# A fused attention and mixer kernel: scores with 128 instead of 112 stationary columns of k, and k kept ahead of q in its tile

## The chip, the cores and the metric

The kernel runs on one core of a Trainium2 chip. The metric is the device time of one execution in microseconds; the time of a kernel is the median of its runs. The page called "the profile" describes one such execution, taken by the hardware profiler: its span goes from the first to the last instruction. PE is TensorE's matmul stream, PEld its weight loads, DVE is VectorE, ACT is ScalarE, POOL is GpSimd and SP is SyncE, which issues most of the DMAs.

## The reference

Two layers follow each other. The first is attention with normalised queries and keys, over 8 batches of 12 heads with 448 positions and 64 channels a head:

```
q_n, k_n = rmsnorm(q, g_q), rmsnorm(k, g_k)          # over the 64 channels
scores   = q_n @ k_n^T / 8                            # 448 x 448 for each head
attn     = exp(scores - max) / (sum(exp(...)) + 1e-9)
x        = attn @ v                                   # heads side by side: 448 x 768 a batch
```

The second is a mixer over `x`: a low-rank mixing of the positions (`U` is 448 x 32, `V` is 32 x 448), then a two-layer perceptron over the channels:

```
u   = x + (x^T @ U @ V)^T
out = u + relu(u @ w_ch1) @ w_ch2                     # 768 -> 3072 -> 768
```

## The kernel before

The 448 positions of a head are laid on 112 partitions with four positions each (`SP = 112`, `NJ = 4`). A group `t` is four heads (24 groups in all), a pair `p` is two heads (48 pairs, six a batch). Pairs are the unit of attention: the 64 channels of the first head lie on partitions 0 to 63 and those of the second on 64 to 127.

For a group, `load` (L187) brings q and k by SP's DMA queue, `squares` (L217, ScalarE or GpSimd) and `reduce` (L227, VectorE) form the sums of squares, `rsqrt` (L234, ScalarE) their inverse roots, and `scale` (L239, VectorE) writes the normalised q and k of one pair as bfloat16 into a tile `qkn`. The index `s` runs over the two tensors in all of them. `transposes` (L250) turns `qkn` into `qkT`, a tile of 128 partitions by 2 by 448: for the first `NPE = 14` pairs by eight TensorE transposes and two VectorE evictions (L258 multiplies q by the gains, L259 copies k), and for later pairs by a DMA transpose (L261), after which `gains` (L263) multiplies q in place.

`scores` (L267) takes chunks of 112 keys as the stationary operand and all 448 queries as the moving one. For each chunk `kc` it issues two weight loads and two matmuls, one for each head of the pair, on the two halves of the partitions; each head has a PSUM bank of its own in the tile `sc` (two tiles of two banks each, pool `ps_s`). `expo` (L277) has ScalarE take the exponential of both heads at once, from PSUM to the bfloat16 tile `E`, one instruction for each chunk. `values` (L281) multiplies `E` (112 keys by 128 queries as the stationary operand) by v with a column of ones appended, so that the last column of the result is the sum of the exponentials; VectorE takes its reciprocal and scales (L302 to L306). The maximum isn't subtracted.

The mixer follows for each batch: `mix_t` and `mix_u` (L317 to L339) for the low-rank part, where `mix_t` uses 32 stationary columns, then `mlp` (L471). Its first product (`ph`, L477) has 128 x 128 stationary tiles of `w1b` and 384 or 512 moving columns; ScalarE and VectorE share the evictions with the relu (L480, L482). The second (L404, tiles `po`, `pa`, `pb`, `pe`) works on 384 columns at a time, with sums and differences of blocks so that seven products do for eight.

The order of the work is written out by hand. `head` (L573) issues the loads, the set-up and all of batch 0's attention; there `scores` is called for single chunks, and short runs of unused matmuls (`heat`, L737) fill gaps on TensorE. From then on `weave` (L725) interleaves the perceptron of batch `b` with the attention of batch `b + 1`: the perceptron is a generator that yields after each block of TensorE work, and each item of `attention` (L505) has a weight that says how much of that work goes before it. There `scores` is called with two chunks at a time, twice a pair, and its four matmuls stand between blocks of the perceptron. The last batch's perceptron has nothing woven in. Each engine works through its instructions in the order in which they were issued.

Of the kernel before, what the change touches and what calls it, by code (L numbers as in the profile page):

```python
# [9 lines left out]
FP32 = mybir.dt.float32  # L10
# [3 lines left out]
OP = AluOpType  # L14
# [3 lines left out]
def kernel(  # L18
# [13 lines left out]
    nc = tc.nc  # L32
    B, H, S, D = q.shape
# [5 lines left out]
    P = 128  # L39
    NJ = 4  # L40
    SP = S // NJ
# [4 lines left out]
    PAD = 64  # L46
# [21 lines left out]
    ps_s = ctx.enter_context(tc.tile_pool(name="ps_s", bufs=2, space=bass.MemoryType.PSUM))  # L68
# [17 lines left out]
    gg = consts.tile([P, 1], FP32, name="gg")  # L86
# [25 lines left out]
    def E_of(p):  # L112
        return Es[p % 3 if p < 6 else p % 2]
# [71 lines left out]
    qks, vts, sqs, rstds, qkns, qkTs, scs, x3_of = {}, {}, {}, {}, {}, {}, {}, {}  # L185

    def load(t, parts=1, ss=(0, 1)):  # L187
        b, h0, n = t // 3, (t % 3) * HG, HG // parts
        for s in ss:
            if t in (2, 3):  # L190
                qks[t, s] = spare[0:SP, t - 2, s]
            elif (t, s) in ((1, 1), (5, 1)):
                qks[t, s] = k1
            else:
                qks[t, s] = loads.tile([SP, HG, NJ * D], FP32, tag="qk", name="qk", bufs=3)
        for h in range(0, HG, n):
            for s in ss:
                nc.sync.dma_start(qks[t, s][:, h:h + n],
                                  (q, k)[s][b, h0 + h:h0 + h + n].rearrange("h (p j) d -> p h (j d)", j=NJ))

    def load_v(t):
        b, h0 = t // 3, (t % 3) * HG
# [47 lines left out]
    def transposes(p):  # L250
        qkn = qkns[p].rearrange("p s j h d -> p (s j) (h d)")
        qkT = attn.tile([P, 2, S], BF16, tag="qkT")
        qkTs[p] = qkT
        if p < NPE:
            pt = ps_mm.tile([P, 2, S], BF16, tag="mm")
            for i in range(2 * NJ):
                nc.tensor.transpose(pt.rearrange("d s (j p) -> d (s j) p", j=NJ)[:, i, :], qkn[:, i, :], ident[:SP, :SP])
            nc.vector.tensor_scalar(qkT[:, 0], pt[:, 0], gg, None, OP.mult)  # L258
            nc.vector.tensor_copy(qkT[:, 1], pt[:, 1])  # L259
        else:  # L260
            nc.sync.dma_start_transpose(qkT.rearrange("d s (j p) -> d (s j) p", j=NJ), qkn)  # L261

    def gains(p):  # L263
        if p >= NPE:
            nc.vector.tensor_scalar(qkTs[p][:, 0], qkTs[p][:, 0], gg, None, OP.mult)  # L265

    def scores(p, kcs):  # L267
        qT, kT = qkTs[p][:, 0], qkTs[p][:, 1]
        for kc in kcs:
            sc = ps_s.tile([SP, 2, 512], FP32, tag="s")  # L270
            for hh in range(2):
                pp = slice(hh * D, (hh + 1) * D)
                nc.tensor.matmul(sc[:, hh, 0:S], kT[pp, kc * SP:(kc + 1) * SP], qT[pp, :],  # L273
                                 start=True, stop=True)
            scs[p, kc] = sc

    def expo(p, kc):  # L277
        nc.scalar.activation(E_of(p)[:, :, PAD + kc * S:PAD + (kc + 1) * S], scs.pop((p, kc))[:, :, 0:S],  # L278
                             AF.Exp, scale=float(D) ** 0.5)

    def values(p, hh):  # L281
# [223 lines left out]
    def attention(b, extra={}):  # L505
# [11 lines left out]
        for p in range(b * 6, b * 6 + 6):  # L517
            t, odd = divmod(p, 2)
            more, more2 = t + 1 < NT, t + 2 < NT
            add(2 if p == 6 else 1, scores, p, (0, 1))  # L520
            add(0, expo, p, 0)
            add(.5, expo, p, 1)
            if p + 1 < NP and (p + 1 >= NPE or not odd):
                add(.5, transposes, p + 1)
# [16 lines left out]
            if odd and p > 6:  # L541
                if 6 <= t + 2 < NT:
                    add(0, load, t + 2, 1, (1,))
                    add(0, load_v, t + 2)
                if t + 3 < NT:
                    add(0, load, t + 3, 1, (0,))
            add(1, scores, p, (2, 3))
            add(0, expo, p, 2)
            add(.5, expo, p, 3)
            if p + 1 < NPE and odd:  # L550
                add(.5, transposes, p + 1)
            if 7 <= p <= 10:
                add(0, mix_u, 0, p - 7, (1,))
            if p + 1 < NP:
                add(0, gains, p + 1)
# [17 lines left out]
    def head():  # L573

        A, Bh = slice(0, 2), slice(2, 4)
        load(0, 2)
        load(1)
        load(2)
# [16 lines left out]
        gain()  # L595
        reduce(0, Bh, (1,))
        transposes(0)
        heat(3)
        squares(1, ALL, (0,), nc.gpsimd)
        rsqrt(0, Bh)  # L600
        scores(0, (0, 1))
        fill = {n: [] for n in range(24)}

# [184 lines left out]
```

## Time and profile before

| | |
|---|---|
| median of 4 runs | 587.05 us (586.18 to 592.49) |
| profiled execution, whole time | 592.49 us |
| its span, from the first to the last instruction | 590.70 us |
| TensorE matmuls (PE) busy | 570.6 us, 97% of the span, 4613 instructions |
| weight loads (PEld) busy | 315.6 us, 4613 instructions |
| VectorE, ScalarE, GpSimd busy | 397.6, 279.7, 77.3 us |
| score matmuls (L273) | 384, mean 384 ns; 48 of them in the first 50 us |
| score weight loads (L273) | 384, mean 126 ns |
| exponentials (L278, `E`) | 184, mean 915 ns; ScalarE idle before them 58.3 us |
| granted TensorE clock | 0.988 of full speed on average; half speed for a while in the first 40 us |

A row of the group table names the line, the engine and the operation, then the tiles (output, arrow, inputs), the shape and the count; behind the first bar stand the busy time in us and the mean duration of one in ns, behind the second the time in us for which the engine was idle just before, with what ended that wait. "issue" means that it waited for nothing that the profile shows. The timeline gives the start of a merged row of instructions, its duration, both in us, and how many they are. The chain gives the start, the duration and the name of pieces of work on the path that ended last. The ends of matmuls are modelled, and matmuls overlap, so the distance between two starts says more than a duration does.

### The profile page before, as it was taken

The numbers are of one execution on the slowest core, as the hardware profiler recorded it, in microseconds if no ns is written. First come the engines' busy times: TensorE is split into PE (matmuls) and PEld (weight loads), VectorE is DVE, ScalarE is ACT, GpSimd is POOL, SyncE is SP. The second block draws the span as 40 slices with busy tenths as digits, with TensorE's granted clock in tenths as the row PEclk, the third lists the DMA queues.
The fourth block names the chain that finished last, engine by engine and source line by source line (L and its number), as shares of the span: only waits on it lengthen the run. The fifth ranks groups of instructions, "written<-read, shape, count | busy, mean of one in ns | idle before, by whom it ended". The sixth has DMA issues, their size and how long they took to land.

```text
span 590.7 us, 11372 instructions
## 1 busy us (share of the span) xinstructions
PE 570.6 (97%) x4613; PEld 315.6 (53%) x4613; DVE 397.6 (67%) x811; ACT 279.7 (47%) x413; POOL 77.3 (13%) x122
## 2 busy tenths in 40 slices
PE   6899999999999999999999999999999999999997
PEld 2465556544455455644455555644455555654464
DVE  5867987389875688747677488757667487453452
ACT  5764664076531776165641676246651476302200
POOL 4751421000120000000020000000001000000010
PEclk9789999999999999999999999999999999999999
DMA  9999997515454355635736355546425441050021
GB/s 207 231 241 235 186 187 153 136 48 97 110 146 98 81 96 137 157 88 110 124 80 126 85 114 123 150 109 126 88 58 157 98 95 33 28 108 0 1 50 58
DMA packets 103648, 67.22 MB, mean 114 GB/s; under 512 B 54716, under 2 KB 102060, under 8 KB 103596
## 3 DMA queue, kind: packets, MB, share of 16 engines
q1 hardware_dynamic: 93988, 56.77, 42.5%
q0 software_dynamic: 9376, 9.44, 9.9%
q8 instruction: 36, 0.59, 0.4%
q10 hardware_dynamic: 232, 0.30, 0.2%
q14 instruction: 16, 0.13, 0.1%
HBM read 52.19 MB, written 11.01 MB: 107 GB/s over the span
## 4 chain that ended last, share of the span: by engine, by line
PE 79%; DVE 9%; DMA 6%; ACT 3%; issue 1%; POOL 0%; DVEq 0%; POOLq 0%; ACTq 0%
PE ph L477 32%; PE pb L404 9%; PE po L404 8%; PE o L299 7%; PE pa L404 7%; PE sc L273 6%; PE pe L404 6%; DMA Tw<-in_k_dram 4%; DVE qkn L244 2%; PE pu L337 2%; ACT E L278 2%; DMA qkT<-qkn 1%; DVE rstd L231 1%; PE warm L741 1%; DVE hT L400 1%
## 5 line engine op out<-in xcount | busy, mean ns | idle before, releaser
L477 PE MATMUL ph<-u,w1b 128*128 128x512 bf16 (+1 forms) x1128 | 232.5, 353 | 0.9 <-DMA u<-x 0.8
L278 ACT ACTIVATE E<-sc 112x896 bf16<-112x896 f32 x184 | 159.4, 915 | 58.3 <-PE sc L273 56.7
L477 PEld LDWEIGHTS <-w1b 128*128 128x128 bf16 x1128 | 103.0, 98 | 107.0 <-issue 20.8
L404 PEld LDWEIGHTS <-hT 128*128 128x128 bf16 x1080 | 101.5, 98 | 71.2 <-issue 7.5
L480 ACT ACTIVATE hT<-ph 128x384 bf16<-128x384 f32 (+1 forms) x95 | 51.7, 546 | 148.4 <-PE ph L477 146.3
L482 DVE TENSOR_SCALAR hT<-ph 128x512 bf16<-128x512 f32 (+1 forms) x93 | 57.9, 623 | 58.8 <-PE ph L477 58.2
L299 PEld LDWEIGHTS <-E 112*128 112x128 bf16 x1472 | 59.8, 99 | 18.0 <-DVE xs L306 3.1
L273 PE MATMUL sc<-qkT 64*112 64x448 bf16 x384 | 62.0, 384 | 5.9 <-DVE qkT L265 2.1
L299 PE MATMUL o<-va,E 112*128 112x65 bf16 x1440 | 62.5, 196 | 1.6 <-DVE xs L306 1.6
L244 DVE TENSOR_TENSOR qkn<-qk,rstd 112x512 bf16<-112x512 f32 x84 | 55.9, 703 | 7.0 <-ACT rstd L237 3.8
L404 PE MATMUL po<-w2b,hT 128*128 128x384 bf16 x288 | 52.0, 326 | 0.6 <-DVE hT L482 0.6
L702 POOL COPY scratch<-qkn 1x1 bf16<-1x1 bf16 x44 | 10.3, 234 | 316.4 <-DVE qkn L244 311.9
L231 DVE TENSOR_REDUCE rstd<-sq 112x16 f32<-112x1024 f32 x40 | 48.5, 1212 | 4.6 <-ACT sq L223 3.9
L404 PE MATMUL pa<-w2b,hT 128*128 128x384 bf16 x264 | 49.5, 326 | 0.0
L404 PE MATMUL pb<-Tw,hT 128*128 128x384 bf16 x264 | 48.0, 326 | 0.0
L273 PEld LDWEIGHTS <-qkT 64*112 64x112 bf16 x384 | 19.6, 126 | 38.3 <-issue 32.3
L223 ACT ACTIVATE sq<-qk 112x1024 f32<-112x1024 f32 x36 | 38.3, 1064 | 0.4 <-ACT hT L480 0.4
L302 DVE RECIPROCAL rec<-o 128x4 f32<-128x4 f32 x96 | 17.1, 178 | 30.6 <-PE o L299 30.5
L303 DVE TENSOR_TENSOR x<-o,rec 128x192 bf16<-128x192 f32 x96 | 34.3, 357 | 3.7
L439 POOL TENSOR_TENSOR o<-o,x 128x384 f32<-128x384 f32 x11 | 12.6, 1146 | 163.7 <-DVE o L438 163.7
L419 ACT ACTIVATE pb<-pa 128x384 f32<-128x384 f32 x11 | 5.2, 474 | 50.2 <-PE pa L404 50.2
L339 DVE TENSOR_TENSOR x<-pu,x 128x768 bf16<-128x768 f32 (+1 forms) x27 | 23.3, 865 | 7.2 <-PE pu L337 7.0
(106 smaller groups left out, 451.4 us busy)
## 6 DMA issues: line engine op xcount, KB each, us to landing
qk<-in_q_dram SPq DMA_DIRECT2D x21, 448.0 KB, 6.1
vt<-in_v_dram SPq DMA_DIRECT2D x20, 448.0 KB, 4.8
qk<-in_k_dram SPq DMA_DIRECT2D x19, 448.0 KB, 3.8
w2b<-in_moe_w_ch_dram POOLq DMA_DIRECT2D x6, 768.0 KB, 9.7
w1b<-in_moe_w_ch_dram POOLq DMA_DIRECT2D x2, 1536.0 KB, 22.5
out_dram<-o SPq DMA_DIRECT2D x15, 168.0 KB, 2.4
out_dram<-o SPq DMA_DIRECT2D x16, 144.0 KB, 2.2
out_dram<-o SPq DMA_DIRECT2D x15, 120.0 KB, 2.0
```

Source lines behind the costliest of these rows:

```text
L223: nc.scalar.activation(sqs[t, s][:, hs], qks[t, s][:, hs], AF.Square)
L231: nc.vector.tensor_reduce(rstds[t][:, s, hs].rearrange("p h j -> p (h j)"), sqs[t, s][:, hs].rearrange("p h (j d) -> p (h j) d", d=D), AX, ...
L244: nc.vector.tensor_tensor(qkn[:, s].rearrange("p j h d -> p h j d"), qks[t, s][:, hp].rearrange("p h (j d) -> p h j d", d=D), rstd[:, s, h ...
L273: nc.tensor.matmul(sc[:, hh, 0:S], kT[pp, kc * SP:(kc + 1) * SP], qT[pp, :], start=True, stop=True)
L278: nc.scalar.activation(E_of(p)[:, :, PAD + kc * S:PAD + (kc + 1) * S], scs.pop((p, kc))[:, :, 0:S], AF.Exp, scale=float(D) ** 0.5)
L299: nc.tensor.matmul(o[:, i, :], E[:, hh, c:c + P], va[:, hl, kc, :], start=(kc == 0), stop=(kc == NJ - 1))
L303: nc.vector.tensor_tensor(x3[:, :, d0:d0 + D], o[:, t0:t0 + 3, 0:D], rec[:, t0:t0 + 3].rearrange("p c -> p c ()").to_broadcast([P, 3, D]), ...
L339: nc.vector.tensor_add(xv, pu[rows, 0:n, 0:HALF], xv)
L404: nc.tensor.matmul(ps, lhs[:, c, :], rhs[:, c, :], start=first and c == 0, stop=last and c == NC - 1, skip_group_check=again)
L477: nc.tensor.matmul(ph, w1b[:, dc, hc * P:(hc + 1) * P], u[:, dc, :], start=(dc == 0), stop=(dc == KD - 1))
L480: nc.scalar.activation(hT[:, hc, 0:n], ph, AF.Relu)
L482: nc.vector.tensor_relu(hT[:, hc, 0:n], ph)
```

## The change

The two tensors change places: index `s` 0 is now k and 1 is q, in the loads, in `qkn` and in `qkT`. With k first, the last chunk of keys can be read 128 columns wide, since 16 columns of q follow it in the tile. `scores` takes 128 stationary columns for each chunk instead of 112, that is its own 112 keys and the 16 columns after them; the score tile has 128 partitions instead of 112. The last 16 rows of each result are not read: `expo` takes partitions 0 to 111. The gains still go to q.

```diff
--- before.py
+++ after.py
@@ -196,7 +196,7 @@
         for h in range(0, HG, n):
             for s in ss:
                 nc.sync.dma_start(qks[t, s][:, h:h + n],
-                                  (q, k)[s][b, h0 + h:h0 + h + n].rearrange("h (p j) d -> p h (j d)", j=NJ))
+                                  (k, q)[s][b, h0 + h:h0 + h + n].rearrange("h (p j) d -> p h (j d)", j=NJ))
 
     def load_v(t):
         b, h0 = t // 3, (t % 3) * HG
@@ -255,27 +255,27 @@
             pt = ps_mm.tile([P, 2, S], BF16, tag="mm")
             for i in range(2 * NJ):
                 nc.tensor.transpose(pt.rearrange("d s (j p) -> d (s j) p", j=NJ)[:, i, :], qkn[:, i, :], ident[:SP, :SP])
-            nc.vector.tensor_scalar(qkT[:, 0], pt[:, 0], gg, None, OP.mult)
-            nc.vector.tensor_copy(qkT[:, 1], pt[:, 1])
+            nc.vector.tensor_scalar(qkT[:, 1], pt[:, 1], gg, None, OP.mult)
+            nc.vector.tensor_copy(qkT[:, 0], pt[:, 0])
         else:
             nc.sync.dma_start_transpose(qkT.rearrange("d s (j p) -> d (s j) p", j=NJ), qkn)
 
     def gains(p):
         if p >= NPE:
-            nc.vector.tensor_scalar(qkTs[p][:, 0], qkTs[p][:, 0], gg, None, OP.mult)
+            nc.vector.tensor_scalar(qkTs[p][:, 1], qkTs[p][:, 1], gg, None, OP.mult)
 
     def scores(p, kcs):
-        qT, kT = qkTs[p][:, 0], qkTs[p][:, 1]
+        qT, kT = qkTs[p][:, 1], qkTs[p].rearrange("d s n -> d (s n)")
         for kc in kcs:
-            sc = ps_s.tile([SP, 2, 512], FP32, tag="s")
+            sc = ps_s.tile([P, 2, 512], FP32, tag="s")
             for hh in range(2):
                 pp = slice(hh * D, (hh + 1) * D)
-                nc.tensor.matmul(sc[:, hh, 0:S], kT[pp, kc * SP:(kc + 1) * SP], qT[pp, :],
+                nc.tensor.matmul(sc[:, hh, 0:S], kT[pp, kc * SP:kc * SP + P], qT[pp, :],
                                  start=True, stop=True)
             scs[p, kc] = sc
 
     def expo(p, kc):
-        nc.scalar.activation(E_of(p)[:, :, PAD + kc * S:PAD + (kc + 1) * S], scs.pop((p, kc))[:, :, 0:S],
+        nc.scalar.activation(E_of(p)[:, :, PAD + kc * S:PAD + (kc + 1) * S], scs.pop((p, kc))[0:SP, :, 0:S],
                              AF.Exp, scale=float(D) ** 0.5)
 
     def values(p, hh):
```

## The prediction

> **What bounds the kernel now.** I read the page's busy table and its chain first, to see which engine sets the end.
>
> ```profile
> PE 570.6 (97%) x4613; PEld 315.6 (53%) x4613; DVE 397.6 (67%) x811; ACT 279.7 (47%) x413; POOL 77.3 (13%) x122
> PE 79%; DVE 9%; DMA 6%; ACT 3%; issue 1%; POOL 0%; DVEq 0%; POOLq 0%; ACTq 0%
> ```
>
> TensorE is busy 97% of the span and makes 79% of the chain that ended last, so a nanosecond taken out of its stream in the woven stages counts nearly whole. That is not so in the first 52 us, where the stage table gives PE 43.5 us busy of 52 and the DMA engines are full; there I count half.
>
> Next the groups of instructions, for the four kinds of weight load and the score matmuls that the edit touches.
>
> ```profile
> L477 PEld LDWEIGHTS <-w1b 128*128 128x128 bf16 x1128 | 103.0, 98 | 107.0 <-issue 20.8
> L299 PEld LDWEIGHTS <-E 112*128 112x128 bf16 x1472 | 59.8, 99 | 18.0 <-DVE xs L306 3.1
> L273 PE MATMUL sc<-qkT 64*112 64x448 bf16 x384 | 62.0, 384 | 5.9 <-DVE qkT L265 2.1
> L273 PEld LDWEIGHTS <-qkT 64*112 64x112 bf16 x384 | 19.6, 126 | 38.3 <-issue 32.3
> ```
>
> A load of 128 columns takes 98 ns, whether it has 128 rows or 112. The score load, with fewer columns (112), takes longer, 126. And it sits idle before it 38.3 us "on issue", waiting for nothing that the profile names. What that idle time is decides the size of the gain, so I went to the timeline, in short windows, so that the four matmuls of one `scores` call come apart (start, duration):
>
> ```profile
> 218.60 0.33 PE L477 MATMUL ph<-u,w1b 128*128 128x384 bf16 x1
> 218.85 0.40 PE L273 MATMUL sc<-qkT 64*112 64x448 bf16 x2
> 218.85 0.13 PEld L273 LDWEIGHTS <-qkT 64*112 64x112 bf16 x2 [0.32 <-issue]
> 219.09 0.35 PE L273 MATMUL sc<-qkT 64*112 64x448 bf16 x2
> 219.37 0.34 PE L477 MATMUL ph<-u,w1b 128*128 128x384 bf16 x1
> ```
>
> Both heads of a pair start together. The first pair lasts 393 ns by record, the second 349. A 384-column matmul is followed by the next of its kind after 1.95/12 = 0.1625 us (chain: twelve `po` in 1.95), yet the first score load comes 0.25 us after `ph`: a hole of 254 - 160 = 94 ns (exact records). From first to second pair there are 230 ns; 448 columns stream in 448/384 x 160 = 187, so the first pair stood about 44 ns, just the 393 - 349. Those 44 ns are its weights arriving with nothing streaming. The second pair's loads start 43 ns after the first pair's and are covered. After the second pair there are 278 - 187 = 91 ns of hole again. So one call pays 94 + 44 + 91 ns beside its two streams.
>
> [...] the operand records of L477, L299 and L404 read 32 x 4 elements, those of L273 read 112 x 1. Price: where a 128-column load is exposed, after a hole, its matmul lasts 336 instead of 326 ns (384 columns), thus 10 ns against the 44 of the 112-column load. [...] Both holes stand where 128-row matmuls meet 64-row ones, [...]. The trace can tell, for one place has the 128-column form on both sides and still changes the rows:
>
> ```profile
> 24.32 0.26 PE L169 MATMUL pt<-ident,Tw 32*128 32x32 bf16 x4
> 24.52 0.61 PE L741 MATMUL warm<-xs 128*128 128x512 bf16 x1
> ```
>
> L169's loads are 32 rows by 128 columns, read 32 x 4. Its last matmul starts at 24.40, the next load at 24.51: 110 ns, of which 32 columns at the half clock of that stage are 27. Some 83 ns of hole remain, as after a score call at that clock (545 - 373 - 93 = 79). The reverse is there too: from L357 (128 rows x 32 columns) to scores, slow form on both sides, the next load starts 158 ns after a 53 ns stream. So I take the holes to stay. This is one instance, at another clock; hence a rival below.
>
> **The change, part by part.** *Loads of 128 columns.* 384 instructions before, 384 after; the exposed part of a load goes from 44 to about 10 ns, a gain of 34 if both heads' loads overlap as now (their records start 3 ns apart), and 24 if the second queues behind the first. I take 30, and keep 17 (44 less two and a half fast loads) and 34 as ends. How many pairs are exposed:
>
> ```profile
> L273 PE MATMUL sc<-qkT 64*112 64x448 bf16 x320 | 48.1, 371 | 4.4 <-DVE qkT L265 2.1 <-DVE rec L302 2.1
> ```
>
> This is the group between 65 and 510 us: a mean of 371 between 349 and 393 says half of them. Counted one by one: of the 160 pairs there 72 have both matmuls long and 14 one (86 exposed), of the 8 between 52 and 65 us 5, of the 24 before 52 us 23, nine of these at half clock (617 ns records, about 60 ns to gain each). Gain: 86 x 30 = 2.6 us; 5 x 30 = 0.15; head (14 x 30 + 9 x 60)/2 = 0.5. Sum 3.2 us. Part of the score calls doesn't wait for its weights at all but for data: PE idles 4.4 us ahead of L273 between 65 and 510 us (DVE's gain and reciprocal, as the line says), in about a tenth of the 80 calls; what is saved just before is given back to that wait. Times 0.88: **2.8 us**.
>
> *Streaming.* The moving operand stays 448 columns, so no matmul gets longer; 16 more rows of the score bank are written and not read. ACT still reads 112 partitions: 0.913 us each, unchanged. Score tiles are two full banks before and after; no buffer changes.
>
> *k ahead of q.* The fourth chunk of k reads 16 columns into q. Its matmul streams q anyway, so nothing new is waited for; from pair 14 on, the weight load rather than the matmul would meet DVE's gain at L265, 2.1 us in 4 waits now, the same event. Built, the two kernels have the same instruction order and waits on PE, DVE, ACT and POOL. On SP's queue the same 211 entries stand in the same order with q's and k's transfers exchanged, equal in size (448 KB, landing in a median 6.1 and 3.8 us); both are needed before a scale can finish. The gain multiply stays first of the two evictions (both wait for the eighth transpose). Zero, covered by that sameness. Were the early q half to land later than k's did, up to 2.3 us (6.1 - 3.8) in a head with a 23.8 us DMA link on the chain; I keep 1 us of it for the range on both sides.
>
> *Against the profiled execution:* span 590.70, whole time 592.49, 1.79 around it. 592.49 - 2.8 = 589.7. That execution is the slowest of four; their median is 587.05, 5.4 lower, with no trace of a faster one. The woven stages should be alike, so the same 2.8 comes off: **584.2 us**, -0.5%.
>
> **Rivals.** *No gain (12%).* The load of a 64-row tile isn't quicker with 128 columns, or waits on ACT and DVE take it all. For: ACT idles only 58.3 us before its exponentials, and they turn round the two score buffers. Against: L169's 32-row loads, exposed, lengthen their matmul by only 204 - 183 = 21 ns at half clock. 587.0 us.
>
> *The holes go too (6%).* If it were the change of load form [...], both holes of a call would vanish: 84 woven calls x (94 + 91) = 15.5 us, plus 1.5 of the head's 24 single calls at half weight and the 2.8: about 567 us. For: in all 84 calls form and rows change together. Against: L169 to L741.
>
> *The heads no longer run side by side (9%, slower).* Place: L273, between the first head's matmul and the second head's load. [...] if the second head's load can't enter while the first head streams, each pair lasts two streams: 192 x 187 = 36 us, some 620 us. It decides once 3.2/0.187 = 17 pairs are split, and only beyond 48 is it over 1%. [...] No row of before shows two row tiles with 128-column loads.
>
> *The forecast, 73%:* 582 to 588.
>
> **How the numbers follow.** A measurement of this kernel can tell about 1% from no change: below 581.2 is faster, above 592.9 slower. Faster: the 6% of the holes and 6 of the forecast's 73 (noise, the head's clock): 0.12. Slower: 9% and 2 of an unlucky draw like the 592.49 above: 0.11. Same: 0.77. Forecast and no gain together hold 85%; the range is theirs: low end 584.2 less 1.2 (34 and no discount) less 1 (head) less 1.5 = 580.5; high end no gain plus 1 plus 1.5 = 589.5. The 1.5 is for the draw: the middle two of four runs are 586.23 and 587.87, so a median moves by 0.8, and there are two of them. The 567 and 620 us cases lie outside it, with 15%, as do some 5% at the edges of the likely ones.
>
> **What would show it.** Score loads at about 98 ns instead of 126; score matmul records near 360 in the first pair, so a mean near 355 instead of 371 in the woven stage; first pair to second 0.20 us instead of 0.23; the holes of 0.25 and 0.28 us before and after unchanged; PE's busy total some 3 us lower. Wrong if the gap from `ph` to the first score load falls to 0.16 us (holes gone), if the second head's matmul starts 0.19 us after the first (heads in series), or if first pair to second stays 0.23 (no quicker load).

## The result, and the profile after

The changed kernel takes 586.35 us in the median of 43 runs (583.59 to 588.58), the kernel before 587.63 us in that of 64 (585.41 to 593.09). Runs compared with runs give a ratio of 0.9965, with a 95% interval of 0.9952 to 0.9977: 0.35% or 2.06 us less (1.35 to 2.82). The two medians lie only 1.28 us apart, the two means 2.08 us: 11 runs of the kernel before took more than 590 us and none of the changed kernel did, so part of the difference could be a matter of luck with the granted clock. The experiments below settle that. The time lies in the range and on the forecast's side, a change of well under 1%. The 2.8 us forecast are somewhat more than was found, at the edge of the interval. The range (580.5 to 589.5) held the case of no gain as well, so that lying in it proves little; what supports the forecast are its signs in the trace.

The busy table, the clock and the score groups of the profile after:

```profile
PE 563.7 (96%) x4613; PEld 308.0 (53%) x4613; DVE 396.2 (68%) x811; ACT 279.2 (48%) x413; POOL 78.9 (13%) x122
...
PEclk9999999999999999999999999999999999999999
...
PE 80%; DVE 9%; DMA 4%; ACT 3%; SPq 2%; issue 1%; DVEq 0%; ACTq 0%
...
L273 PE MATMUL sc<-qkT 64*128 64x448 bf16 x384 | 56.6, 357 | 7.0 <-DVE rec L302 2.6
...
L273 PEld LDWEIGHTS <-qkT 64*128 64x128 bf16 x384 | 13.0, 94 | 39.0 <-issue 32.0
```

The score load fell from a mean of 126 ns to 94 although it has 16 columns more, and the score matmul from 384 to 357. The idle time on "issue" ahead of the score loads, 32.3 us before, is 32.0: the holes are still there. The bound is the same engine. PE's busy total fell by 6.9 us instead of the forecast 3: 2.7 us of that lie behind the first `first` matmul (L714, the start of the perceptron's first product at the end of the head), and 4.2 ahead of it.

The timeline of one woven score call, in the form in which the prediction shows it for the kernel before:

```profile
213.85 0.33 PE L477 MATMUL ph<-u,w1b 128*128 128x384 bf16 x1
214.11 0.36 PE L273 MATMUL sc<-qkT 64*128 64x448 bf16 x2
214.11 0.10 PEld L273 LDWEIGHTS <-qkT 64*128 64x128 bf16 x2 [0.32 <-issue]
214.31 0.35 PE L273 MATMUL sc<-qkT 64*128 64x448 bf16 x2
214.59 0.34 PE L477 MATMUL ph<-u,w1b 128*128 128x384 bf16 x1
```

The first pair's records went from 0.40 to 0.36 us (393 to 359 ns); first pair to second takes 0.20 us instead of 0.24 (199 ns instead of 233, start of the first head to start of the first head). From `ph` to the first score matmul it is 0.25 to 0.26 us as it was, from the last score matmul to `ph` 0.28, so both holes stand. The two heads of a pair start 4 ns apart (3 before).

**Where the time went.** All 4613 matmuls start in the same order in both traces, so the lag of each matmul behind its twin can be followed through the program. At the end it is 5.57 us in these two executions, but only 1.92 us of it (539.83 us instead of 541.75) arose in the woven stage and after. The other 3.64 lie ahead of the first `first` matmul, in the head:

```profile
L714 PE MATMUL first<-u,w1b x24: 323/326/337, 44.8 to 51.2; 128*128 128x384 bf16 x24
```

for the kernel before, and for the kernel after

```profile
L714 PE MATMUL first<-u,w1b x24: 322/326/337, 41.1 to 47.6; 128*128 128x384 bf16 x24
```

(the two numbers after the durations are the first and the last start). TensorE was granted half its clock for 13.65 us of the head in the execution before (21.6 to 35.3 us), 3.41 us in that after (28.4 to 31.8). Two profiled executions alone would thus have shown nearly three times the gain. Other executions of the same woven stage repeat the 1.92: from the first `first` matmul to the last of the program it takes 541.98, 541.75 and 540.88 us in the three profiled executions with 112 columns there, 539.83, 539.76 and 539.16 in the three with 128 (the designs are below).

For the rest of the account I summed, over the 84 woven score calls of each kernel, the time from the end of the stream before the call to the start of the next matmul that isn't a score. That end is an estimate from the trace of before: perceptron matmuls of 512 columns mostly start 215 or 216 ns apart, those of 384 columns 162 or 163, so 128 columns stream in about 53 ns, and the stream is taken to end 160 ns after its start for 384 columns, at other widths in proportion. Each row is one profiled execution:

```
kernel                            sum, us   hole before   first to last start   hole after   (medians, ns)
before                            58.26         96              237                95
after                             56.18         99              203                95
order only (112 columns)          58.20         96              237                95
128 columns in chunks 0 to 2      56.33         98              203                95
128 columns, pairs 6 to 47 only   55.57         99              203                95
128 columns, pairs 0 to 5 only    57.95         96              237                95
127 columns                       58.28         96              244                95
after, with a 128-row matmul      74.53         99              461               105
after, with a 64-row matmul       59.05         98              256                95
after, more filling in the head   56.65         99              203                95
```

The change takes 34 ns out of the middle of a call and adds 3 in front (both loads now start before the first matmul, 4 and 1 ns in the median; before, the second started 2 ns after it): 84 x 31 = 2.6 us. The sum fell by 2.08; single executions with one width of the load differ in it by 0.3 us with 112 columns and by 1.1 with 128. Waits of second pairs beyond the median grew from 1.52 to 1.95 us, and this repeats (1.52 or 1.53 in the other executions with 112 columns, 1.92 to 1.95 in those with 128 and nothing put in between). Waits beyond the median hole before a call went from 4.80 to 5.20, but range from 4.5 to 4.8 and from 4.6 to 5.7 in the same executions. So some of the saving was given back to waits for ScalarE and VectorE. One such call, before and after:

```profile
197.13 0.80 PE L273 MATMUL sc<-qkT 64*112 64x448 bf16 x4 [0.56 <-DVE qkT L265]
```

```profile
193.03 0.77 PE L273 MATMUL sc<-qkT 64*128 64x448 bf16 x4 [0.62 <-DVE qkT L265]
```

TensorE comes 60 ns earlier and waits 60 ns longer for VectorE's gain.

### The profile page after: what moved, and what is told of

Its sections match the earlier page's. It is cut to its first block, busy times and chain, and to the rows that moved or that the text cites. A ratio compares the mean times of both kernels' runs of the same rounds, so it can differ in the third digit from the quotient of the medians.

```text
span 585.1 us, 11372 instructions
## 1 busy us (share of the span) xinstructions
PE 563.7 (96%) x4613; PEld 308.0 (53%) x4613; DVE 396.2 (68%) x811; ACT 279.2 (48%) x413; POOL 78.9 (13%) x122
## 4 chain that ended last, share of the span: by engine, by line
PE 80%; DVE 9%; DMA 4%; ACT 3%; SPq 2%; issue 1%; DVEq 0%; ACTq 0%
PE ph L477 32%; PE pb L404 9%; PE po L404 8%; PE o L299 8%; PE pa L404 7%; PE pe L404 6%; PE sc L273 6%; DMA hT<-in_q_dram 2%; ACT E L278 2%; DVE qkn L244 2%; PE pu L337 2%; DMA qkT<-qkn 1%; DVE hT L400 1%; DVE S L399 1%; SPq L198 1%
## 5 line engine op out<-in xcount | busy, mean ns | idle before, releaser
L273 PE MATMUL sc<-qkT 64*128 64x448 bf16 x384 | 56.6, 357 | 7.0 <-DVE rec L302 2.6
L702 POOL COPY scratch<-qkn 1x1 bf16<-1x1 bf16 x44 | 11.5, 262 | 310.7 <-DVE qkn L244 309.0
L273 PEld LDWEIGHTS <-qkT 64*128 64x128 bf16 x384 | 13.0, 94 | 39.0 <-issue 32.0
```

The source lines that it names most:

```text
L273: nc.tensor.matmul(sc[:, hh, 0:S], kT[pp, kc * SP:kc * SP + P], qT[pp, :], start=True, stop=True)
```

## The experiments

The theory: the gain is the exposed part of a weight load (44 ns with 112 columns and 10 with 128 in the two traces), and it takes the full 128. The rivals: the order of q and k; wider columns by degrees; the head; and holes that belong to the width of the load.

**The order alone.**

```diff
 # the change, with
-            sc = ps_s.tile([P, 2, 512], FP32, tag="s")
+            sc = ps_s.tile([SP, 2, 512], FP32, tag="s")
-                nc.tensor.matmul(sc[:, hh, 0:S], kT[pp, kc * SP:kc * SP + P], qT[pp, :],
+                nc.tensor.matmul(sc[:, hh, 0:S], kT[pp, kc * SP:(kc + 1) * SP], qT[pp, :],
```

> The change with k ahead of q, but 112 stationary columns as before. Theory (the time comes from weight loads that stand exposed: 44 ns with 112 columns, 10 ns with 128): ratio to the kernel before 1.000 within 0.002; score loads 123 ns, first pairs of matmuls 393 ns, so none of the 2 us. Rival (the order of q and k, in the transfers or in the tile, gives the gain): ratio about 0.9965.

Measured: ratio 0.9995 (0.9974 to 1.0017); the score calls take 58.20 us against 58.26 before. The exchange of q and k costs and brings nothing that can be seen, to within 0.2 to 0.3%.

**128 columns where the tile allows it, q ahead of k.**

```diff
 # the kernel before, with
-            sc = ps_s.tile([SP, 2, 512], FP32, tag="s")
+            sc = ps_s.tile([P, 2, 512], FP32, tag="s")
+            n = P if kc < 3 else SP
-                nc.tensor.matmul(sc[:, hh, 0:S], kT[pp, kc * SP:(kc + 1) * SP], qT[pp, :],
+                nc.tensor.matmul(sc[0:n, hh, 0:S], kT[pp, kc * SP:kc * SP + n], qT[pp, :],
-    ... scs.pop((p, kc))[:, :, 0:S]
+    ... scs.pop((p, kc))[0:SP, :, 0:S]
```

> q stays ahead of k as in the kernel before; chunks 0 to 2 have 128 stationary columns, chunk 3, behind which the tile ends, has 112. Theory: in the woven stage chunk 3 is always in the second pair of a call, whose loads are mostly covered by the first pair's stream, so nearly the whole gain comes without the exchange: ratio 0.9965 to 0.998, chunk-3 loads 123 ns, the other loads 93, and the exposed first pairs at 360. Rival (k ahead of q is needed, or a change between two forms of load costs a hole of its own): ratio 1.000 or above, and the gap from first pair to second near 0.29 us instead of 0.20.

Measured: ratio 0.9965 (0.9946 to 0.9984), the change's own ratio, without the exchange. The groups between 60 and 500 us, then one call whose second chunk is the 112-column one:

```profile
L274 PE MATMUL sc<-qkT 64*128 64x448 bf16 x238 | 37.3, 356 | 5.2 <-DVE qkT L265 2.5 <-DVE rec L303 2.2
L274 PE MATMUL sc<-qkT 64*112 64x448 bf16 x78 | 13.7, 349 | 0.0
L274 PEld LDWEIGHTS <-qkT 64*112 64x112 bf16 x78 | 5.4, 136 | 0.0
```

```profile
220.29 0.36 PE L274 MATMUL sc<-qkT 64*128 64x448 bf16 x2
220.49 0.35 PE L274 MATMUL sc<-qkT 64*112 64x448 bf16 x2
```

The slow loads of chunk 3 are still slow (136 ns, 123 were expected) and cost nothing: their matmuls last 349 ns in the mean, the value of a covered load. So these slow loads cost nothing where they are covered, and 44 ns where the trace of before has them exposed (393 - 349). The two rows of the call also settle the change between two widths of load: 128-column and 112-column matmuls follow each other in 0.20 us (199 ns, as 128 follows 128 in the kernel after), so a change from 128 to 112 columns opens no hole; from 112 to 128 was not run.

**The woven stage alone, and the head alone.**

```diff
 # the change, with one of
+            n = P if p >= 6 else SP
 # and
+            n = P if p < 6 else SP
 # and in both
-                nc.tensor.matmul(sc[:, hh, 0:S], kT[pp, kc * SP:kc * SP + P], qT[pp, :],
+                nc.tensor.matmul(sc[0:n, hh, 0:S], kT[pp, kc * SP:kc * SP + n], qT[pp, :],
```

> The change, but the six pairs of batch 0, in the head, keep 112 stationary columns; pairs 6 to 47 have 128. Theory: the gain is in the woven stage, about 1.9 us: ratio 0.9968. Rival (the gain of the medians is the head's, through its clock or its waits): ratio 1.000.

> The change, but only the six pairs of batch 0 have 128 stationary columns; pairs 6 to 47 keep 112. Theory: at most 0.5 us, ratio 0.999 to 1.000, and the woven stage from the first of its score calls on keeps its pace to 0.1 us. Rival (the head's gain is what the medians show): ratio 0.9965.

Measured: ratio 0.9968 (0.9948 to 0.9989) with 128 columns in the woven stage alone, 1.0006 (0.9987 to 1.0024) with them in the head alone. The gain is that of the woven stage. A gain in the head of more than 0.8 us is excluded; whether there is one of a few tenths stays open, since the first `first` matmul comes anywhere between 38.8 and 41.1 us in those of these executions whose head kept its clock or nearly so. The loads did shorten the head's calls (at full clock 292 instead of 326 ns from the last score matmul to the next one), but what that saved is mostly or wholly waited for again; for what was not traced. The second run's pace after the head was not kept to 0.1 us as expected: the 541.98 us above are its time, against 541.75 before and 540.88 with the order alone. So single executions with 112 columns differ by about 1 us there, and the 1.92 us have that uncertainty.

The granted clock is not the cause of the gain. Among the runs taken together with these two, with a mean granted clock of 0.999 or more, the kernel before has a mean of 587.05 us (38 runs), the order alone 586.8 (10) and the head alone 586.7 (6); 128 columns in the woven stage alone have 585.05 (15), in chunks 0 to 2 585.1 (14). The 2 us are there at full clock too.

**127 columns.**

```diff
 # the change, with
+            n = P - 1
-                nc.tensor.matmul(sc[:, hh, 0:S], kT[pp, kc * SP:kc * SP + P], qT[pp, :],
+                nc.tensor.matmul(sc[0:n, hh, 0:S], kT[pp, kc * SP:kc * SP + n], qT[pp, :],
```

> The change with 127 stationary columns instead of 128. Theory (only a full 128 columns are loaded in the quick form; otherwise the exposed load grows with its columns): exposed load 44 x 127/112 = 50 ns, first pairs near 399 ns, [...] some 115 exposed pairs x 6 ns = 0.7 us slower than the kernel before, ratio 1.001. Rival (wider columns help by degrees, or what helps is reading past the chunk's end): first pairs near 360 ns and ratio 0.9965.

Measured: ratio 1.0028 (0.9993 to 1.0062). One column less and the gain is gone, as the group (60 to 500 us) and a call show:

```profile
L274 PE MATMUL sc<-qkT 64*127 64x448 bf16 x316 | 48.1, 375 | 3.9 <-DVE rec L303 2.1 <-DVE qkT L265 1.6
L274 PEld LDWEIGHTS <-qkT 64*127 64x127 bf16 x316 | 16.1, 132 | 30.0 <-issue 28.4 <-DMA qkT<-qkn 0.9
```

```profile
225.09 0.40 PE L274 MATMUL sc<-qkT 64*127 64x448 bf16 x2
225.33 0.35 PE L274 MATMUL sc<-qkT 64*127 64x448 bf16 x2
```

The exposed first pairs last 401 ns, so 52 ns of load are exposed against 44 with 112 columns and 10 with 128. Of the three widths run, 112, 127 and 128, only 128 has the short load (126, 132 and 94 ns in the mean), so it is not width by degrees.

**What the holes are.** Two runs put one more matmul into each of the 84 woven calls, between its two chunks; the chunk's own scores overwrite its result. Both stream 128 columns. The first has 128 rows, the second 64:

```diff
 # the change, with one of
+            if p >= 6 and kc % 2:
+                nc.tensor.matmul(sc[:, 0, 0:P], ident, ident, start=True, stop=True)
 # and
+            if p >= 6 and kc % 2:
+                nc.tensor.matmul(sc[:, 0, 0:P], kT[0:D, 0:P], qT[0:D, 0:P], start=True, stop=True)
```

> The change, and in each of the 84 woven score calls one more matmul of 128 rows and 128 moving columns between the first and the second chunk; its result is overwritten by the chunk's own scores. Theory (the holes are the array's change between 128-row and 64-row tiles): it opens two more holes a call, 84 x (53 ns stream + 98 + 94 + about 20 of exposed loads) = 22 us, some 608 us. Rival (holes belong to something else at the start and end of a call, such as the tile's wait): 84 x 53 ns to 84 x 75 ns = 4 to 6 us, some 591 us.

> The change, and in the same place one more matmul of 64 rows (the first head's half) and 128 moving columns, whose result is overwritten. Theory: no change of tile rows, so no hole: 84 x (53 ns, plus up to 10) = 4.5 to 5.3 us over the change, some 591 us. Rival (any matmul more in the call breaks its pairs apart and costs holes): 608 us, like the 128-row one.

Measured: 602.67 us in only two runs, ratio 1.0224 (1.0141 to 1.0308), with the 128-row matmul, so neither the expected 608 nor the rival's 591; 589.87 us, ratio 1.002 (0.999 to 1.0051), with the 64-row one. A call with the 128-row matmul:

```profile
226.42 0.36 PE L275 MATMUL sc<-qkT 64*128 64x448 bf16 x2
226.72 0.23 PE L272 MATMUL sc<-ident 128*128 128x128 bf16 x1
226.88 0.36 PE L275 MATMUL sc<-qkT 64*128 64x448 bf16 x2
227.18 0.34 PE L406 MATMUL po<-w2b,hT 128*128 128x384 bf16 x1
```

and with the 64-row one:

```profile
220.41 0.36 PE L275 MATMUL sc<-qkT 64*128 64x448 bf16 x2
220.61 0.22 PE L272 MATMUL sc<-qkT 64*128 64x128 bf16 x1
220.61 0.40 PE L275 MATMUL sc<-qkT 64*128 64x448 bf16 x2
220.95 0.34 PE L406 MATMUL po<-w2b,hT 128*128 128x384 bf16 x1
```

Pair to pair takes 0.46 us with the 128-row matmul instead of 0.20, with a hole on either side of a 53 ns stream. With the 64-row one the first head of the second pair starts right behind it, 0.20 us after the first pair as without it; the next perceptron matmul comes 0.54 us after the first pair instead of the 0.48 in the call of the kernel after. All loads of both calls have 128 columns, so the hole belongs to the change between 128-row and 64-row tiles. The median calls grew by 258 + 10 = 268 ns and by 53 ns; by expectation 265 and 53 to 63. The whole times grew by less than 84 times that, 16.3 and 3.5 us over the median of the change. For the 128-row matmul it is 22.5 us by the calls' medians and 18.35 in the sum of the calls, since waits at the second pairs (1.95 us before, 0.24 now) and ahead of the calls (5.20, now 2.78) took up 4.1; for the 64-row one 4.4 and 2.87.

**More filling in the head.**

```diff
 # the change, with
-            for _ in range(n):
+            for _ in range(n if n >= NWARM else 2 * n):
```

> The change, with twice as many of the unused matmuls that fill TensorE's gaps in the head (19 more than before, each about 0.215 us). Theory of the spread (the profiled run of before had half the clock for 13.65 us of its head, that of after for 3.41 us, and 3.6 of the 5.6 us between the two spans lie there): a clock of 1.000 throughout and a median near 584.5, ratio 0.9945. Rival (the extra matmuls stand in the way of the head's transposes and scores): slower than the change by up to 19 x 0.215 = 4 us, ratio 1.003.

Measured: 587.20 us, ratio 0.998 (0.9961 to 0.9999), so neither the expected 0.9945 nor the rival's 1.003. It is not faster than the change alone; its median is 0.85 us higher, but the intervals of the two ratios overlap and the two weren't run side by side. The clock was kept: 18 of 20 runs have a mean of 0.999 or more, 19 of 44 for the change, and the profiled execution (mean 0.998) never had half the clock before its last 4 us. But its first pair of batch 1 came at 52.1 us, where five other profiled executions without half the clock and without an extra matmul had it at 50.5 to 51.2. So the time that the clock gives seems to go to the extra matmuls; the two weren't measured apart. No version is clearly faster than the changed kernel.

## Why the prediction was right, point by point

- **The bound.** TensorE's stream in the woven stage sets the end, and a change of 34 ns a call reached it: right. A share of it stays behind in waits.
- **44 ns exposed against 10.** Measured 44 (393 - 349) against 10 (359 - 349). The 30 ns assumed for a pair turned out as 34 less the 3 that the second load adds in front of the first matmul, 31. Both loads start 3 ns apart, so the end of 17 ns did not arise.
- **The number of exposed pairs.** Woven 2.75 us was forecast before the discount; the medians of the calls give 2.6.
- **The discount for waits, 0.88.** This is the term that was mis-sized. The sum of the calls fell by 2.08 us and the woven stretch by 1.92, thus 0.70 to 0.76 of the forecast 2.75. The mechanism was named: what is saved just before is given back at the next wait. Its size was not: a tenth of the calls was priced as losing its own saving, while a waiting call also gives back what calls before it saved. Of the seven calls whose second pair waits most, none kept the 34 ns: from first to last start, three took 407 or 408 ns before and 409 to 411 after, and four grew by 30 to 32 ns, three of them from 456 to 487 or 488. Ahead of three other calls the hole grew from 725 or 726 ns to 786 to 789.
- **The head, 0.5 us before the discount.** The loads shortened, a gain in time was not seen: 1.0006 with the columns in the head alone. Its interval doesn't exclude it either.
- **k ahead of q costs nothing.** Right within the interval, 0.9995.
- **The holes stay.** Right, and on the evidence of one place: the trace of before has a change from 32 to 128 rows with 128-column loads on both sides, at half clock, and some 83 ns of hole there. The 128-row and 64-row matmuls then showed it at full clock 84 times over: with a 128-row matmul in its middle a call takes 258 ns longer from first to last start, with a 64-row one 53. In the traces of before and after a change from 128 to 64 rows or back leaves 95 to 99 ns in the median. What TensorE does in that time, no trace shows.
- **The rivals.** No gain: excluded by the interval, and by the loads' 94 ns. Heads one after the other, whose 9% was an estimate with no row of before for or against it: the second starts 4 ns after the first, both with a 128-column load of 94 ns in the mean. Holes that go too: they stood.
- **The level.** The forecast started from a median of four runs, 587.05; over 64 runs it is 587.63. That is 0.6 us which no step of the sum could know. The 586.35 measured are 2.1 us above the 584.2 forecast: these 0.6, 0.7 by which the gain was smaller, and 0.8 by which the medians lie closer together than the ratio says.

## What to carry to other kernels

In these traces a score call's weight loads cost time only where nothing streams over them, which is in its first pair, after the change from 128-row to 64-row tiles; there, at full clock, 128 columns exposed 10 ns, 112 exposed 44 and 127 exposed 52. So where such loads are many and exposed, a stationary operand a little short of 128 is worth widening over whatever lies beside it, if the extra rows are never read; where the loads are covered, as in chunk 3 above, it brings nothing. The larger cost at such a place is the change of tile rows itself, 95 to 99 ns each way, which neither width of load removed; fewer changes should, but that was not run. And compare engine records at the same instruction in both traces before trusting the difference of two spans: here two thirds of it lay in a stretch of the head where the granted clock differed.

## What the runs showed that I had not expected

- The granted clock goes with as much time as the change brings. Of 44 executions of the changed kernel, the 13 with a mean granted clock of 1.000 took a median of 585.1 us, the 12 at or below 0.994 took 587.4; the correlation of clock and time is -0.73. In the two profiled executions with half the clock before their last 4 us, one of each kernel, that was in the head; for runs without a trace only the mean is known. What brings the half clock on was not shown.
- The second pair's loads start early, although they go to the tile rows of the running matmuls: in the median 11 ns after the first pair's first matmul started with 128 columns, 47 ns with 112.
- The woven stage swallowed part of each of the three changes in TensorE's work followed here, in both directions: of 2.6 us saved 2.1 showed in the sum of the calls, of 22.5 us added 18.4, of 4.4 added 2.9.
